# GpSimd's product of a unit's query features with the reciprocals in two halves, all low halves on VectorE, the sums of keys masked, and a new table of order corrections

## The chip, the cores and the metric

The kernel runs on one core of a Trainium2 chip. The metric is the device time of one execution in microseconds (us), the median of several runs: 1688.12 us over three runs of the kernel before (1687.51 to 1689.02). Five engines work side by side, each through its own queue in a fixed order: PE (TensorE, matrix products), DVE (VectorE), ACT (ScalarE), POOL (GpSimd) and SP (SyncE, which here issues all transfers). An instruction that has to wait holds up everything behind it on its engine.

## The reference

Two attention layers over 2048 tokens, 1024 wide, 32 heads of 32, whose outputs are laid side by side. Layer A works in four segments of 512 tokens: causal softmax attention inside a segment, plus a memory that is carried from segment to segment. Layer B is linear attention with learned features:

```python
pq = einsum("bhsd,hdf->bhsf", q, w_phi)            # the same for k
phi_q = concat([softmax(pq), softmax(-pq)], -1)    # 64 features a head
phi_k = concat([softmax(pk), softmax(-pk)], -1)
kv = einsum("bhsf,bhsd->bhfd", phi_k, v);  z = einsum("bhsf->bhf", phi_k)
o = einsum("bhqf,bhfd->bhqd", phi_q, kv) / (phi_q . z + 1e-6)
```

Then `o @ wo`. The change touches layer B's `kv` and its queries.

## The kernel before

Every large product is done with operands split into a high and a low half of 16 bits (high times high, high times low, low times high), so nearly every tile that PE reads has been written twice: ACT writes the high half, then DVE or POOL writes the low half as the difference of the value and its high half. Products of 1024 by 1024 by a pair of token tiles are done with seven block products (`strassen`, line 618 for the matmuls, 624 and 628 for the sums between them).

Four stages follow one another on PE. **Units** (to about 900 us): 32 units of layer A (four heads of a segment each), with the projections of the next unit (line 404), the scores twice (lines 882 and 983, once for the maxima, which DVE reduces at line 888, and once for the exponentials, lines 987 to 990) and the product with the values (line 1019). Between them lies work in advance for layer B: folded weights, and the prepared forms of pairs of token tiles (`prepare`, whose maxima DVE takes at line 1174). **Keys** (to about 1205 us): for each of eight pairs of token tiles the key features and values of layer B, summed into `kva` and `ez` (line 1444) and `za`. **Queries** (to about 1540 us): 16 token tiles c, each in two half-units hb of 16 heads. **Output** of layer A (line 1681) to the end.

A half-unit of the queries is a chain. PE's `strassen` gives the scores; DVE takes maxima and minima (1274), subtracts them (1276, 1278), ACT takes exponentials (1281), DVE sums them and takes reciprocals (1284, 1287). POOL multiplies with the sums of keys `zb` (1587, two instructions), DVE reduces (1590), three small steps of POOL and DVE give the reciprocal of the denominator (1593 to 1598), POOL multiplies the features `e` with these reciprocals (1600, one instruction over 1024 columns), ACT writes the high half into `S` (1607, two instructions of 512), and the low half is written by line 1610, two instructions of 512: by DVE, but for the first two token tiles the second of the two by POOL. SP then issues a transposing transfer into `pt` (1613), and PE multiplies with `kls` (1622, 48 small matmuls). After both half-units ACT and DVE bring the result out of PSUM into `ot` (1631, 1633) and PE projects it (line 404, 48 matmuls a token tile).

`kls` is `kva` and `ez`, each multiplied with reciprocals of the sums of keys (`zr`, lines 1471 to 1476), in two halves of 16 bits (1478, 1480). Its blocks hold two heads by two heads; line 1622 reads only the two blocks on the diagonal.

The order of every queue is worked out in Python when the program is built. Each `op(...)` names its engine, an assumed duration, what it reads and writes, and a due number `prio`. `Graph.run` then goes through the engines, and of the instructions that could start earliest on one it takes that of the lowest due number. Instructions with the same due number that follow each other in the text are a job; a table `MOVES` adds a correction to the due numbers of single jobs on single engines:

```python
        if prio != self.job[0]:
            self.job = prio, self.job[1] + 1
        prio += MOVES.get(eng, {}).get(self.job[1], 0.0)
```

Of the kernel before, what the change touches and what calls it, by code (L numbers as in the profile page):

```python
# [8 lines left out]
F32 = mybir.dt.float32  # L9
# [67 lines left out]
    "ACT": {  # L77
# [6 lines left out]
    "POOL": {  # L84
        42: 1, 95: -4, 100: -5, 147: 2, 148: -1.5, 150: -5, 161: 0.5, 173: 12, 188: 7, 222: -21.5, 240: 2.6, 245: 0.5,
        250: -1.5, 255: -2.5, 257: -2.5, 264: -5.5, 270: -5, 282: -22.5, 326: -8, 328: 2, 341: -2.5, 376: 10.5, 389: -36.5},
# [205 lines left out]
def tile_kernel(ctx: ExitStack, tc: tile.TileContext, ax, aw, awv, awo, beta, bx, bwqk, bwv, bphi, bwo, out):  # L292
# [37 lines left out]
    nc.vector.memset(one, 1.0)  # L330
    pst = const.tile([128, NT // 2, 5], F32, name="pst")
# [958 lines left out]
    def bc32(r):  # L1290
        return r()[:, :, :, None].to_broadcast([128, 16, 2, 32])
# [177 lines left out]
    for hb in range(2):  # L1469
        zr, v = G.buf("b", [128, 8], F32, "zr", 2), slice(8 * hb, 8 * hb + 8)  # L1470
# [5 lines left out]
        op(DVE, 0.62, lambda zr=zr, hb=hb: nc.vector.tensor_tensor(  # L1476
            kva[hb](), kva[hb](), zr()[:, :, None].to_broadcast([128, 8, 64]), op=OP.mult), r=[zr], w=[kva[hb]], prio=P, port=True)
# [75 lines left out]
    for c in range(NT):  # L1553
# [28 lines left out]
        for hb in range(2):  # L1582
            e, r = er[c % 2, hb]
            dn = G.buf("b", [128, 16, 2], F32, "dn", 2)
            for a in range(2):
# [14 lines left out]
            op(POOL, 1.95, lambda e=e, r=r: nc.gpsimd.tensor_tensor(e(), e(), bc32(r), op=OP.mult),  # L1600
               r=[e, r], w=[e], prio=P)
# [4 lines left out]
            for q in range(2):  # L1606
                op(ACT, 0.53, lambda q=q, e=e, hv=hv: nc.scalar.activation(
                    hv()[:, 0, 512 * q:512 * q + 512], ev(e)[:, 512 * q:512 * q + 512], AF.Copy), r=[e], w=[(eh, (hb, 0, q))], prio=P)
                sub, ns, d = (POOL, nc.gpsimd, 1.28) if q and c < 2 else (DVE, nc.vector, 0.7)
                op(sub, d, lambda q=q, e=e, hv=hv, ns=ns: ns.tensor_tensor(  # L1610
                    hv()[:, 1, 512 * q:512 * q + 512], ev(e)[:, 512 * q:512 * q + 512], hv()[:, 0, 512 * q:512 * q + 512], op=OP.subtract),
                   r=[e, (eh, (hb, 0, q))], w=[(eh, (hb, 1, q))], prio=P, port=True)
# [140 lines left out]
```

## Time and profile before

| | us |
|---|---|
| median of 3 runs | 1688.12 |
| the profiled execution, whole | 1690.85 |
| its span, from first to last instruction | 1689.1 |
| PE busy in it | 1658.1 |
| DVE busy | 1344.2 |
| ACT busy | 1157.4 |
| POOL busy | 966.5 |

The profiled execution is 2.7 us longer than the median; sums below are made against it and then carried to the median as differences. Busy time of PE counts a matmul to its modelled end, so a PE that is busy is not always one at full pace. The second part of the page shows the busy share of each engine in 40 slices and the clock that PE was granted; a table by stretches of time, asked of the trace, shows what each engine did in each stage.

### The profile page before, as it was taken

To read this page: it belongs to the slowest core of one execution; us is meant where nothing else is said; L and a number is where in the kernel's file an instruction comes from. 1 tells how busy PE (TensorE), PEld (TensorE's weight loads), DVE (VectorE), ACT (ScalarE), POOL (GpSimd) and SP (SyncE) were. 2 spreads that over 40 slices of the span, in tenths; PEclk is the share of its full clock that TensorE was granted. 3 is DMA by queue.
4 is the path that set the end of the run, shared out by engine and by line. 5 is a ranking of instruction groups with operands and counts; after the bars stand their busy time and mean duration, and the time that the engine had idled before them with its cause. 6 is when DMAs were issued, how large, how long until landed. Compare 5 with 4: busy or idle time off the path is not lost. (4 is left out here: it accounts for less than half of the span.)

```text
span 1689.1 us, 40231 instructions
## 1 busy us (share of the span) xinstructions
PE 1658.1 (98%) x15176; PEld 995.5 (59%) x15176; DVE 1344.2 (80%) x3198; ACT 1157.4 (69%) x2128; POOL 966.5 (57%) x1285
## 2 busy tenths in 40 slices
PE   8999999999999999999999999999979999999999
PEld 6767667666767767767764454454534444444444
DVE  6889898888998878878974787877978896976441
ACT  7898989878878988777873486765545564454331
POOL 4346578546468885756661576754588888450000
PEclk9999999999999999999999999999989999999999
DMA  7556646655766484864367465467546775865311
GB/s 224 170 170 165 211 141 195 210 174 160 243 195 191 140 223 126 224 188 127 93 179 265 150 219 168 139 205 282 207 97 166 173 202 136 220 140 169 124 57 62
DMA packets 261970, 292.64 MB, mean 173 GB/s; under 512 B 138880, under 2 KB 192896, under 8 KB 255120
## 3 DMA queue, kind: packets, MB, share of 16 engines
q1 hardware_dynamic: 261776, 290.07, 57.5%
q8 instruction: 119, 1.95, 0.5%
q14 instruction: 75, 0.61, 0.1%
HBM read 161.17 MB, written 86.05 MB: 146 GB/s over the span
## 5 line engine op out<-in xcount | busy, mean ns | idle before, releaser
L404 PE MATMUL proj<-S,S 128*128 128x512 f16 (+1 forms) x3072 | 504.3, 300 | 2.8 <-ACT S L437 1.1
L404 PEld LDWEIGHTS <-S 128*128 128x128 f16 x4608 | 333.8, 98 | 154.0 <-issue 7.4
L618 PE MATMUL proj<-S,S 128*128 128x512 f16 x1584 | 362.7, 379 | 0.6 <-ACT cs L624 0.6
L618 PEld LDWEIGHTS <-S 128*128 128x128 f16 x2016 | 192.8, 98 | 220.4 <-issue 1.8
L996 POOL TENSOR_SCALAR_AFFINE_SELECT ph<-ph 128x256 f16<-128x256 f16 (+1 forms) x448 | 192.1, 451 | 139.1 <-DVE ph L990 113.4
L888 DVE CUSTOM_DVE_ANT_0 s<-s,causal 128x256 f32<-128x256 f32 (+3 forms) x512 | 242.7, 509 | 16.7 <-PE s L882 13.3
L990 DVE SCALAR_TENSOR_TENSOR ph<-s,ph 128x512 f16<-128x512 f32 x320 | 209.7, 682 | 40.5 <-ACT ph L989 38.7
L989 ACT ACTIVATE ph<-s 128x512 f16<-128x512 f32 x320 | 189.1, 649 | 0.7
L404 PE MATMUL misc<-S,ot 128*128 128x512 f16 x768 | 175.2, 385 | 0.7 <-ACT ot L1631 0.7
L1281 ACT ACTIVATE e<-e,sk 128x256 f32<-128x256 f32 x256 | 112.3, 496 | 61.5 <-DVE e L1278 59.7
L404 PEld LDWEIGHTS <-ot 128*128 128x128 f16 x768 | 74.4, 99 | 90.7 <-issue 3.4
L983 PE MATMUL s<-S 104*128 104x512 f16 (+3 forms) x512 | 115.7, 299 | 1.9 <-ACT S L910 1.2
L882 PE MATMUL s<-S 96*128 96x512 f16 (+3 forms) x512 | 112.9, 299 | 2.3 <-DVE mt L888 1.4
L987 ACT ACTIVATE s<-s,os 128x512 f32<-128x512 f32 x160 | 105.5, 700 | 13.7 <-PE s L983 13.6
L987 ACT ACTIVATE s<-s,bd 128x512 f32<-128x512 f32 x160 | 106.2, 705 | 7.9 <-PE s L983 6.5
L404 PE MATMUL proj<-wv,S 128*128 128x128 f16 x1536 | 108.4, 219 | 0.0
L1019 PEld LDWEIGHTS <-ph 128*128 128x128 f16 x2560 | 87.1, 96 | 18.0 <-issue 1.9
L1587 POOL TENSOR_TENSOR e<-e,zb 128x512 f32<-128x512 f32 x64 | 84.7, 1341 | 21.8 <-DVE r L1284 18.2
L1019 PE MATMUL pv<-vl,ph 128*128 128x66 f16 (+1 forms) x2560 | 91.9, 184 | 1.0 <-DVE mt L888 0.6
L1284 DVE TENSOR_REDUCE r<-e 128x32 f32<-128x1024 f32 x64 | 76.7, 1205 | 16.3 <-ACT e L1281 16.3
L888 DVE DVE_READ_ACCUMULATOR2_ANT mt<- 128x1 f32 x512 | 72.0, 141 | 0.0
L1393 POOL TENSOR_TENSOR e<-e,r 128x1024 f32<-128x1024 f32 x32 | 61.3, 1920 | 15.4 <-DVE r L1287 11.9
(336 smaller groups left out, 3257.1 us busy)
## 6 DMA issues: line engine op xcount, KB each, us to landing
S<-xf_d SPq DMA_DIRECT2D x126, 256.0 KB
S<-h SPq DMA_DIRECT2D x192, 128.0 KB
S<-wf_d SPq DMA_DIRECT2D x21, 1024.0 KB
st<-bwqk SPq DMA_DIRECT2D x64, 256.0 KB
out<-os SPq DMA_DIRECT2D x40, 256.0 KB
S<-aw SPq DMA_DIRECT2D x16, 512.0 KB
wa_d<-S SPq DMA_DIRECT2D x16, 512.0 KB
wf_d<-fo SPq DMA_DIRECT2D x32, 256.0 KB
```

Source lines behind the costliest of these rows:

```text
L404: op(PE, dur, lambda c=c, a=a, b=b, lv=lv, rv=rv: nc.tensor.matmul(pv(), lv(), rv(), start=(c == 0 and a + b == 0), stop=(c == n - 1 and a ...
L618: op(PE, 0.215, lambda n=n, a=a, b=b, lv=lv, rv=rv: nc.tensor.matmul(ps(), lv(), rv(), start=(start and n == 0 and a + b == 0), stop=(n == ...
L882: nc.tensor.matmul(ps()[:, o:o + 128 * i + 128], st()[0:96, 0, h, 128 * i:128 * i + 128], st()[0:96, 1, h, 0:128 * i + 128], start=True, s ...
L888: dve(0.12 + 0.00113 * n, lambda h=h, i=i, o=o, n=n: nc.vector.tensor_tensor_reduce(ps()[:, o:o + n], ps()[:, o:o + n], causal[:, 512 - n: ...
L983: nc.tensor.matmul(ps()[:, o:o + n], st()[0:104, 1, h, 128 * j:128 * j + 128], st()[0:104, 0, h, 128 * j:512], start=True, stop=True)
L987: act(0.59, lambda: nc.scalar.activation(ps(), ps(), AF.Exp, bias=0.0, scale=bdv()[:, 3, i2, 0:1]), r=[(bd, i2)], w=[ps])
L989: act(0.5, lambda: nc.scalar.activation(ph()[:, 0], ps(), AF.Copy, scale=2.0 ** 14), r=[ps], w=[(ph, 0)])
L990: dve(0.6, lambda: nc.vector.scalar_tensor_tensor(ph()[:, 1], ps(), 2.0 ** 14, ph()[:, 0], op0=OP.mult, op1=OP.subtract), r=[ps, (ph, 0)], ...
L996: nc.gpsimd.affine_select(pd, pd, pattern=[[0, n], [1, 128]], compare_op=OP.is_ge, fill=0.0, base=0, channel_multiplier=-1)
L1019: nc.tensor.matmul(ps()[:, i, n0:n1], ph()[:, a, o:o + 128], vl()[:, j, h, n0:n1], start=(i == 0 and a == 0), stop=(j == min(i, 2)), skip_ ...
L1281: op(ACT, 0.41, lambda i=i: nc.scalar.activation(e()[:, 4 * i:4 * i + 4], e()[:, 4 * i:4 * i + 4], AF.Exp, bias=0.0, scale=sk()[:, i:i + 1 ...
L1587: op(POOL, 1.35, lambda a=a, h0=h0, e=e: nc.gpsimd.tensor_tensor(e()[:, 8 * a:8 * a + 8], e()[:, 8 * a:8 * a + 8], zv()[:, h0:h0 + 8], op= ...
```

## The change

Four edits. First, the product of line 1600 becomes two instructions of 512 columns, and each half of ACT's and DVE's work waits for its own half alone. Second, all low halves of the queries are DVE's. Third, `zr` is multiplied with a mask `bm2` (1 on the two diagonal blocks, 0 elsewhere) into `zs`, a small tile of 8 by 2, and `kva` and `ez` are multiplied with that; the blocks that become zero are those that line 1622 doesn't read. `bm2` itself is one small reduction of DVE at the start. Fourth, the whole table `MOVES` is another one, with 167 entries in place of 234, and so the order of all five queues is worked out anew, from the first units to the end of the queries.

```diff
 MOVES = {
     "DVE": {
-        4: -4.5, 10: -1.5, 15: -4, 27: 0.5, 37: -2, 39: -45.5, 43: -22, 56: 4, 73: 0.6, 81: 7, 88: -43.5, 91: -10, 93: -48.5,
+        4: -3.5, 10: -0.5, 16: 3, 24: -0.7, 27: -0.1, 89: -0.5, 100: -2, 105: -7, 109: 1.5, 121: 0.5, 128: -2, 139: 1.1,
...
+    bm2 = const.tile([128, 2], F32, name="bm2")
+    nc.vector.tensor_reduce(bm2, bm.rearrange("p (two h) -> p two h", two=2), axis=AX.X, op=OP.add)
...
-        op(DVE, 0.62, lambda zr=zr, hb=hb: nc.vector.tensor_tensor(
-            kva[hb](), kva[hb](), zr()[:, :, None].to_broadcast([128, 8, 64]), op=OP.mult), r=[zr], w=[kva[hb]], prio=P, port=True)
+        op(DVE, 0.1, lambda zr=zr, zs=zs: nc.vector.tensor_tensor(
+            zs(), zr()[:, :, None].to_broadcast([128, 8, 2]), bm2[:, None, :].to_broadcast([128, 8, 2]), op=OP.mult),
+           r=[zr], w=[zs], prio=P)
+        op(DVE, 0.62, lambda zs=zs, hb=hb: nc.vector.tensor_tensor(
+            kva[hb]().rearrange("p g (b d) -> p g b d", d=32), kva[hb]().rearrange("p g (b d) -> p g b d", d=32),
+            zs()[:, :, :, None].to_broadcast([128, 8, 2, 32]), op=OP.mult), r=[zs], w=[kva[hb]], prio=P, port=True)
...
-            op(POOL, 1.95, lambda e=e, r=r: nc.gpsimd.tensor_tensor(e(), e(), bc32(r), op=OP.mult),
-               r=[e, r], w=[e], prio=P)
+            for q in range(2):
+                op(POOL, 1.05, lambda q=q, e=e, r=r: nc.gpsimd.tensor_tensor(
+                    e()[:, 8 * q:8 * q + 8], e()[:, 8 * q:8 * q + 8], bc32(r)[:, 8 * q:8 * q + 8], op=OP.mult),
+                   r=[e, r], w=[(e, ("y", q))], prio=P)
...
-                    hv()[:, 0, 512 * q:512 * q + 512], ev(e)[:, 512 * q:512 * q + 512], AF.Copy), r=[e], w=[(eh, (hb, 0, q))], prio=P)
-                sub, ns, d = (POOL, nc.gpsimd, 1.28) if q and c < 2 else (DVE, nc.vector, 0.7)
-                op(sub, d, lambda q=q, e=e, hv=hv, ns=ns: ns.tensor_tensor(
+                    hv()[:, 0, 512 * q:512 * q + 512], ev(e)[:, 512 * q:512 * q + 512], AF.Copy), r=[(e, ("y", q))], w=[(eh, (hb, 0, q))], prio=P)
+                op(DVE, 0.7, lambda q=q, e=e, hv=hv: nc.vector.tensor_tensor(
                     hv()[:, 1, 512 * q:512 * q + 512], ev(e)[:, 512 * q:512 * q + 512], hv()[:, 0, 512 * q:512 * q + 512], op=OP.subtract),
-                   r=[e, (eh, (hb, 0, q))], w=[(eh, (hb, 1, q))], prio=P, port=True)
+                   r=[(e, ("y", q)), (eh, (hb, 0, q))], w=[(eh, (hb, 1, q))], prio=P, port=True)
```

Three places of the new order are shown here, since the prediction rests on them. Line numbers in the rows of the change are its own: 1614 is the transposing transfer (1613 before), 1611 DVE's low half (1610), 1609 ACT's high half (1607), 1170 the maxima of a prepared pair (1174), 986 the low half of the exponentials (990).

**DVE, at the start of the queries.** Before, the rows down to the low halves of the first token tile's second half-unit (its first half-unit's stands 22 rows higher); `mx`, `r`, `d` and `dn` are the small tiles of the chain above, `S` the tile that the transfer reads:

```order
L1595 TENSOR_REDUCE d_19811<-dn 128x16
L1274 TENSOR_REDUCE mx<-proj 128x16 x2
L1284 TENSOR_REDUCE r<-e 128x32
L1274 TENSOR_REDUCE mx<-proj 128x16
L1597 RECIPROCAL d_19811<-d_19811 128x16
L1287 RECIPROCAL r<-r 128x32
L1274 TENSOR_REDUCE mx<-proj 128x16
L1610 TENSOR_TENSOR S_19649<-e,S_19649 128x512
L1480 TENSOR_TENSOR kls<-ez,kls 128x512
L1610 TENSOR_TENSOR S_19649<-e,S_19649 128x512
```

And in the change:

```order
L1283 RECIPROCAL r<-r 128x32
L415 RECIPROCAL wsc<-wsc 128x1
L1270 TENSOR_REDUCE mx<-proj 128x16
L1529 TENSOR_TENSOR wsc<-wsc,osc_109 128x1
L1270 TENSOR_REDUCE mx<-proj 128x16
L1590 TENSOR_REDUCE dn<-e 128x16
L1611 TENSOR_TENSOR S_19616<-e,S_19616 128x512 x4
L1272 TENSOR_TENSOR e<-s,mx 128x16x32
```

All four low halves of the first token tile now stand in one row, and none stands ahead of them.

**SP, at the same place**: the transfers into `pt` among the loads of token forms. Before:

```order
L606 DMA S_13808<-xf_d 128x1024
L1613 DMA_TRANSPOSE pt<-S_19649 128x16x128
L606 DMA S_13808<-xf_d 128x1024
L606 DMA S_15069<-xf_d 128x1024
L1613 DMA_TRANSPOSE pt<-S_19649 128x16x128 x3
L606 DMA S_13808<-xf_d 128x1024 x2
```

And in the change:

```order
L602 DMA S_13941<-xf_d 128x1024 x2
L1614 DMA_TRANSPOSE pt<-S_19616 128x16x128 x2
L602 DMA S_15202<-xf_d 128x1024
L1614 DMA_TRANSPOSE pt<-S_19616 128x16x128 x2
L1500 DMA out<-os 128x512 x2
```

The first token tile's two transfers are now issued one right after the other. On PE 1548 matmuls of line 618 stand ahead of the first 48 of line 1622 where there were 1540; then come 96 of line 1622 and 48 of line 404, where there were 48, 8 more of line 618, 96 and 10.

**DVE, in the units**: the first prepared pair's maxima (`xt`). Before, they stand between the `mh` (line 903) of the fourth unit and that of the fifth:

```order
L902 TENSOR_SCALAR mh<-mt 128x4x4
L1174 TENSOR_REDUCE xt<-S_2044 128x1
L1127 TENSOR_SCALAR quad<-misc,sif 128x512
L990 SCALAR_TENSOR_TENSOR ph<-s,ph 128x512 x2
L1174 TENSOR_REDUCE xt<-S_2044 128x1
L990 SCALAR_TENSOR_TENSOR ph<-s,ph 128x512
```

And in the change, between that of the third and that of the fourth:

```order
L832 SCALAR_TENSOR_TENSOR h_1865<-proj,bd,h_1865 128x512
L1170 TENSOR_REDUCE xt<-S_1925 128x1
L986 SCALAR_TENSOR_TENSOR ph<-s,ph 128x512 x3
L435 SCALAR_TENSOR_TENSOR S_1805<-S_1541,wgs,S_1805 128x512 x2
L1019 TENSOR_REDUCE oall<-pv 128x132
L986 SCALAR_TENSOR_TENSOR ph<-s,ph 128x512 x3
L1170 TENSOR_REDUCE xt<-S_1925 128x1
```

The two instructions have moved one unit ahead, to where unit work and weight halves (line 435, 439 before) already stand. The table moves such work for later stages in most units, on all engines.

More of the change, by code (lines that the diff above doesn't have):

```diff
@@ L58 @@
     "DVE": {
[18 rows of a table removed]
-    "ACT": {
[6 rows of a table removed]
[14 rows of a table added]
+    "ACT": {
[4 rows of a table added]
     "POOL": {
-        42: 1, 95: -4, 100: -5, 147: 2, 148: -1.5, 150: -5, 161: 0.5, 173: 12, 188: 7, 222: -21.5, 240: 2.6, 245: 0.5,
-        250: -1.5, 255: -2.5, 257: -2.5, 264: -5.5, 270: -5, 282: -22.5, 326: -8, 328: 2, 341: -2.5, 376: 10.5, 389: -36.5},
+        73: 0.5, 86: -0.5, 102: -3, 128: -3, 131: 1, 147: 0.1, 201: 0.1, 225: -3, 254: -2, 276: -4, 298: -27, 362: -9.5,
+        365: 1.5, 374: 1, 387: -55.5},
 }
@@ L1469, in tile_kernel @@
     for hb in range(2):
-        zr, v = G.buf("b", [128, 8], F32, "zr", 2), slice(8 * hb, 8 * hb + 8)
+        zr, zs, v = G.buf("b", [128, 8], F32, "zr", 2), G.buf("b", [128, 8, 2], F32, "zs", 2), slice(8 * hb, 8 * hb + 8)
         op(DVE, 0.1, lambda zr=zr, v=v: nc.vector.tensor_scalar(zr(), za()[:, v], 1e-12, None, op0=OP.max),
```

38 rows, old and new, of the table MOVES are left out of this document.

## The prediction

> **What bounds the kernel now.** I read the page's first two parts, then the table by stretches of time, PE's waits, and the timeline where the waits lie.
>
> ```profile
> span 1689.1 us, 40231 instructions
> PE 1658.1 (98%) x15176; PEld 995.5 (59%) x15176; DVE 1344.2 (80%) x3198; ACT 1157.4 (69%) x2128; POOL 966.5 (57%) x1285
> PEclk9999999999999999999999999999989999999999
> ```
>
> PE is busy for 98% of the span, at full clock but for one slice. Only its 31 us of idle time, and what follows from them, can be won; and as PE's work stays the same, whatever a new order adds as idle time is lost. Where the idle time lies is told by the stretches (start:end, length, then busy time of PE, PE's weight loads, DVE, ACT, POOL, granted clock, DMA share, GB/s):
>
> ```profile
> 50.00:200.00 150.00, 149.59 (x1635) 108.82 (x1633) 134.22 (x406) 133.38 (x243) 77.03 (x140) 1.00 0.57 161
> 200.00:300.00 100.00, 95.95 (x1077) 69.04 (x1075) 93.17 (x258) 90.14 (x164) 77.37 (x111) 1.00 0.59 187
> 300.00:900.00 600.00, 595.66 (x6472) 417.92 (x6473) 513.79 (x1470) 491.19 (x877) 389.58 (x592) 1.00 0.59 176
> 900.00:1205.00 305.00, 304.18 (x2078) 153.03 (x2077) 229.74 (x408) 190.66 (x391) 168.76 (x163) 1.00 0.60 205
> 1205.00:1260.00 55.00, 44.41 (x390) 21.36 (x390) 45.77 (x86) 24.31 (x50) 41.65 (x44) 0.88 0.55 150
> 1260.00:1500.00 240.00, 240.00 (x2195) 111.23 (x2194) 202.34 (x335) 125.37 (x242) 182.18 (x190) 1.00 0.69 174
> 1500.00:1550.00 50.00, 47.62 (x394) 21.65 (x393) 35.88 (x56) 22.74 (x37) 9.50 (x12) 0.97 0.61 177
> ```
>
> In the units (50 to 900 us) PE is idle for 0.4 + 4.0 + 4.3 = 8.8 us, nearly half of it between 200 and 300. Keys: 0.8 us. The start of the queries: 10.6 us, the one large hole; their middle: none; their end: 2.4 us. The hole is a wait for transposing transfers:
>
> ```profile
> PE pv L1622 <- DMA pt<-S: 11.3, 3, 7.4
> 1227.00 1.91 SPq L1613 DMA_TRANSPOSE pt<-S  x1
> 1235.69 1.15 POOL L1610 TENSOR_TENSOR S<-e,S 128x512 f16<-128x512 f32 x1
> 1238.70 1.18 DVE L1610 TENSOR_TENSOR S<-e,S 128x512 f16<-128x512 f32 x1
> 1239.94 10.83 SPq L1613 DMA_TRANSPOSE pt<-S  x3
> 1244.54 0.63 PEld L1622 LDWEIGHTS <-kls 64*32 64x32 f16 x48 [7.39 <-issue]
> 1247.61 0.57 PEld L1622 LDWEIGHTS <-kls 64*32 64x32 f16 x47 [2.43 <-issue]
> 1248.38 4.45 PE L404 MATMUL misc<-S,ot 128*128 128x512 f16 x10
> 1502.82 10.53 PE L404 MATMUL misc<-S,ot 128*128 128x512 f16 x48
> ```
>
> The second half-unit's low half by POOL is done at 1236.84; DVE's comes at 1238.70, as DVE's queue has it behind other work. The transfer is issued at 1239.94 and used at 1244.54, 4.6 us later. After the hole ten matmuls take 4.45 us, where 48 take 10.53 (0.22 each): another 2.3 us, by a lower clock. So hole and slow restart cost 7.4 + 2.4 + 2.3 = 12.1 us.
>
> **The change, part by part.**
>
> *The start of the queries.* Up to the row of four low halves DVE has, counted over its order, two L1274 and one each of L1276, L1278, L1284, L1287, L1595, L1597 fewer than up to the late low half now, and no low half ahead of them where there was one; it has one L1480 and the two masks' products more.
>
> ```profile
> L1274 DVE TENSOR_REDUCE mx<-proj 128x16 f32<-128x512 f32 x10 | 6.5, 668 | 0.1
> L1284 DVE TENSOR_REDUCE r<-e 128x32 f32<-128x1024 f32 x5 | 6.0, 1196 | 0.0
> L1278 DVE TENSOR_TENSOR e<-mx,proj 128x512 f32<-128x512 f32 x4 | 2.7, 674 | 0.0
> L1287 DVE RECIPROCAL r<-r 128x32 f32<-128x32 f32 x6 | 1.8, 318 | 0.0
> L1597 DVE RECIPROCAL d<-d 128x16 f32<-128x16 f32 x4 | 0.9, 226 | 0.0
> L1480 DVE TENSOR_TENSOR kls<-ez,kls 128x512 f16<-128x512 f32 x1 | 0.7, 678 | 0.0
> L1476 DVE TENSOR_TENSOR kva<-kva,zr 128x512 f32<-128x512 f32 x1 | 0.9, 903 | 0.0
> L1610 DVE TENSOR_TENSOR S<-e,S x60: 628/710/2396, 1225.3 to 1519.4; 128x512 f16<-128x512 f32 x60
> ```
>
> Less: 2 x 0.67 + 2 x 0.67 + 1.20 + 0.32 + 0.23 + 0.71, and for L1595 no more than the 0.23 of L1597: 5.4 us. More: 0.68, and two products of 16 columns, which the trace doesn't have; between nothing and an L1287 (0.32), I take 0.2 each: 1.1 us. The product of kva itself keeps its 512 columns and so its 0.7 to 0.9. DVE is busy for 45.8 of these 55 us, so the row begins about 4.3 us sooner, at 1234.4, and its four parts, 0.7 each, end at 1235.8 for the first half-unit and 1237.2 for the second. SP issues the first transfer at about 1236 and, 1.9 us later, the second at 1238; 4.6 us on, PE has them at 1240.7 and 1242.8. By now the second is used at 1244.54: 1.7 us won. The wait of 2.43 us for the next tile goes, since 48 matmuls of the projection (10.5 us) now stand ahead of it; but these wait for `ot`, four evictions after the last small matmul, and that wait is open where now 48 small matmuls stand (0.6 us). From 1244.54 to 1248.38 pass 3.8 us now; from 1242.8 the projection begins at 1246.6 at the latest: 1.8 us won, 0.6 of it owed for the 48 that come later. Term: -1.2 us. Bounds: -12.1 if the hole goes altogether, +2.8 if DVE's row is not sooner and its four parts come on top.
>
> A rule of the Trainium skill (page "SBUF — State Buffer", section "SBUF: two separate sides") speaks against this part: a VectorE instruction with two inputs in SBUF and a GpSimd instruction that reads SBUF share one pair of ports, as a lock held for a whole instruction, and the loser stands still. The trace agrees, with 2396 ns at most beside the median 710 in the last row above; had each of the four parts the 0.5 us more of the row at 1238.70, the term would be +0.8.
>
> *The halves on POOL.*
>
> ```profile
> L1600 POOL TENSOR_TENSOR e<-e,r x32: 1903/1912/2363, 1222.3 to 1513.6; 128x1024 f32<-128x1024 f32 x32
> L1587 POOL TENSOR_TENSOR e<-e,zb x64: 1255/1270/1804, 1204.8 to 1498.5; 128x512 f32<-128x512 f32 x64
> L1610 POOL TENSOR_TENSOR S<-e,S x4: 1154/1270/1450, 1225.7 to 1247.7; 128x512 f16<-128x512 f32 x4
> ```
>
> A half of 512 columns costs between 0.96 (half of 1.91) and 1.27 (L1587, as many columns). It is the same operation as L1600, so I take 1.0: 64 x 1.0 - 32 x 1.91 = +3 us on POOL, up to +20 by the other bound, less 4 x 1.27 = 5 for the low halves that leave. Between 1260 and 1500 POOL has 58 of 240 us free and PE waits for nothing: no cost there. What a half-unit wins is that ACT begins one half, 0.9 us, sooner; it counts only where PE waits.
>
> *The end of the queries.*
>
> ```profile
> 1516.33 4.51 PE L404 MATMUL misc<-S,ot 128*128 128x512 f16 x13 [0.70 <-ACT ot L1631]
> ```
>
> The idle 2.4 us and 4.51 - 13 x 0.22 = 1.7 us of slow restart are 4.1 us. In the order of the change POOL's last four halves stand in a row, behind the small steps of both half-units, and 15 matmuls (3.3 us) stand on PE between the last two products where there were 24 (5.3 us). Two half-units that end together, with shorter cover: I take -1.0, bounds -4.1 and +4.
>
> *The new order elsewhere.* PE's idle time in the units is not where ACT or DVE has most to do alone, but where the order leaves no spare:
>
> ```profile
> 100.00:150.00 50.00, 49.69 (x526) 34.23 (x524) 46.10 (x152) 43.22 (x78) 27.38 (x44) 1.00 0.71 183
> 150.00:200.00 50.00, 49.90 (x580) 37.75 (x578) 46.16 (x130) 45.43 (x83) 28.74 (x52) 1.00 0.58 166
> 400.00:450.00 50.00, 49.65 (x514) 35.52 (x513) 48.76 (x151) 40.86 (x76) 26.19 (x48) 1.00 0.73 231
> 450.00:500.00 50.00, 50.00 (x565) 35.68 (x563) 47.29 (x129) 40.17 (x72) 30.20 (x49) 1.00 0.64 183
> L1174 DVE TENSOR_REDUCE xt<-S x10: 1192/1205/1215, 151.2 to 746.5; 128x1 f32<-128x1024 f32 x10
> ```
>
> Three stretches of 100 us have DVE at 92 of 100 or more: 100 to 200 (92.3), 200 to 300 (93.2), 400 to 500 (96.1). The first and the last lose 0.4 and 0.35 us, the middle one 4.0. Only the sequence keeps the two tight ones quiet, and the change draws it anew: the first pair's two maxima (2 x 1.2 us) now at 151 move a unit ahead, into the stretch 100 to 150, onto a DVE with 3.9 of 50 us free. I take it that these two come to lose what 200 to 300 loses: 2 x 4.05 - 0.76 = +7.3 us. Bounds: -8.8 if the new order has no idle time in the units, +25.6 if all 850 us lose 4.05 in 100 (34.4 - 8.8). In keys, middle and output, idle for 0.8 us now, an order can only lose; I take once more the 0.8 of the keys.
>
> Sum: -1.2 - 1.0 + 7.3 + 0.8 = +5.9 us. On the profiled execution (span 1689.1, 1690.85 with what lies around it) that is 1696.8; it stood 2.7 above the median, so on the median 1688.1 it is **1694**.
>
> **The rivals.**
>
> *The order is better, not worse* (faster). The units' chain would lose nothing in the tight stretches and 4 us less between 200 and 300, and the start of the queries half of its 12.1: 1688.1 - 4 - 6 = 1678; with the tail's 1.0, 1677. For it: 31 us of idle time are there, and low halves that no longer wait for both POOL and DVE. Against: POOL's low half was done 1.9 us ahead of DVE's, so it was never POOL that held the transfer. It decides where the first four low halves end before 1232.5, 4.6 us ahead of the time at which PE runs dry now (1244.54 - 7.39 = 1237.1).
>
> *Nothing moves.* The masked blocks have no reader, and the halves serve a chain that PE doesn't wait for in 240 of 300 us; start -1.2, tail -1.0 and a units' loss of 2 cancel: 1688. That the edits don't do what they say is in this case.
>
> *DVE and POOL block one another* (slower still). Low halves between 1260 and 1500 are covered by PE's full queue, but at both ends each of eight loses 0.5 us and POOL's last four halves cost 1.27: 4 + 1.2, on top of the forecast 1694 + 5 = 1699; decided by whether low halves in the row of four exceed 1.1 us.
>
> **How the numbers follow.** Forecast 0.50, faster rival 0.25, nothing 0.17, blocked ports 0.08. A measurement of this kernel tells about 0.2%, 3.4 us, from no change. Forecast and blocked ports lie beyond it: slower 0.58; same 0.17; faster 0.25. The likeliest case's own range is 1691 to 1706. The range has to reach into the faster rival, half of which lies above 1677, and up to half of the units' upper bound (1688 + 20): 1677 to 1708.
>
> **What would show it.** The table by stretches: PE idle above 10 us in 50 to 900, most of it in 100 to 200 and 400 to 500; 8 to 10 us idle around the first transfers, without the second wait; no idle between 1260 and 1500. Low halves in a row near 0.7 us, POOL's halves near 1.0. Wrong it would be if the units' idle time fell below 8.8 us, or if PE's wait for the first transfers were under 4 us or over 11.

## The result and the profile after

| | before | after |
|---|---|---|
| median of 12 runs, us | 1688.87 (1685.5 to 1691.3) | 1692.48 (1690.3 to 1696.6) |
| profiled span, us | 1689.1 | 1691.9 |
| ratio after to before | | 1.0023, 95% interval 1.0014 to 1.0032 |

The changed kernel is slower by 0.23%, 3.6 us; the forecast was 5.9 us. The first lines of its page:

```profile
span 1691.9 us, 40286 instructions
PE 1658.1 (98%) x15176; PEld 994.2 (59%) x15176; DVE 1353.6 (80%) x3205; ACT 1154.9 (68%) x2128; POOL 980.3 (58%) x1313
```

PE is busy for the same 1658.1 us, so the 2.8 us that the span has grown by are idle time. Where it lies is told by the table by stretches (start:end, length, then busy time of PE, weight loads, DVE, ACT, POOL, granted clock, DMA share, GB/s) of the changed kernel:

```profile
50.00:200.00 150.00, 148.79 (x1626) 107.67 (x1624) 129.17 (x391) 126.32 (x231) 74.42 (x135) 1.00 0.51 154
200.00:300.00 100.00, 95.33 (x1002) 68.57 (x1000) 92.21 (x250) 93.67 (x170) 75.59 (x105) 0.98 0.58 180
300.00:500.00 200.00, 193.26 (x2167) 136.37 (x2165) 184.13 (x510) 161.42 (x289) 111.74 (x186) 1.00 0.64 197
500.00:900.00 400.00, 398.09 (x4331) 278.84 (x4330) 332.55 (x969) 324.75 (x584) 274.39 (x405) 1.00 0.56 164
900.00:1205.00 305.00, 304.96 (x2048) 151.77 (x2045) 226.53 (x406) 187.97 (x388) 177.85 (x172) 1.00 0.61 207
1205.00:1260.00 55.00, 45.78 (x380) 24.04 (x379) 53.76 (x102) 28.17 (x57) 35.50 (x41) 0.94 0.57 167
1260.00:1500.00 240.00, 239.52 (x2284) 111.15 (x2283) 206.80 (x334) 127.18 (x247) 194.68 (x218) 1.00 0.69 173
1500.00:1550.00 50.00, 49.18 (x409) 22.46 (x407) 38.73 (x62) 24.50 (x40) 15.68 (x19) 1.00 0.62 173
```

In the units (50 to 900 us) PE is now idle for 1.2 + 4.7 + 6.7 + 1.9 = 14.5 us, 5.7 more than before. At the start of the queries it is 9.2 us (10.6 before), at their end 0.8 (2.4 before), and at both ends the clock stays higher: 0.94 for 0.88 and 1.00 for 0.97. What the queries won is less than what the units lost.

The units also lost some clock, which they had not before: between 200 and 300 us it is 0.98 for 1.00, and all of that lies in the last ten of these (0.83 between 290 and 300), right behind PE's longest wait in the stretch, which ends with ACT:

```profile
PE misc L931 <- ACT oT L670: 1.9, 1, 1.9
```

A clock that is 0.17 short for 10 us is, as an estimate, another 1.7 us lost beside the idle time.

The three places that the forecast spoke of read as follows in the changed kernel. First its timeline at the start of the queries (start, length, instruction): DVE's row of four low halves, POOL's halves beside it, the transfers, and PE's weight loads that wait for them:

```profile
1242.03 4.37 DVE L1611 TENSOR_TENSOR S<-e,S 128x512 f16<-128x512 f32 x4
1242.24 1.50 POOL L1601 TENSOR_TENSOR e<-e,r 128x512 f32<-128x512 f32 x1
1244.36 1.49 POOL L1601 TENSOR_TENSOR e<-e,r 128x512 f32<-128x512 f32 x1
1244.35 4.61 SPq L1614 DMA_TRANSPOSE pt<-S  x2
1248.97 0.47 PEld L1623 LDWEIGHTS <-kls 64*32 64x32 f16 x48 [2.25 <-issue]
1251.77 0.57 PEld L1623 LDWEIGHTS <-kls 64*32 64x32 f16 x47 [2.33 <-issue]
1253.46 1.03 PE L400 MATMUL misc<-S,ot 128*128 128x512 f16 x2 [0.85 <-ACT ot L1632]
1254.91 7.32 PE L400 MATMUL misc<-S,ot 128*128 128x512 f16 x29 [0.42 <-DVE ot L1634]
```

The two waits for transfers are 2.25 and 2.33 us where they were 7.39 and 2.43. They are not the same two: before, the second was for the next token tile, and now it stands between the two half-units of the first. The first two matmuls of the projection take 1.03 us and the 29 behind them 7.32, together 1.5 more than 31 x 0.22; before, ten lost 2.3. But the low halves take 1.09 us each, not 0.7, and each half on POOL beside them 1.5.

Second, the same stretch for PE by what it waited for (total, times, longest):

```profile
PE pv L1623 <- DMA pt<-S: 4.5, 2, 2.3
PE misc L1454 <- DVE za L1440: 1.8, 1, 1.8
PE proj L614 <- ACT cs L620: 1.4, 2, 0.8
PE misc L400 <- ACT ot L1632: 0.9, 1, 0.9
```

So 5.2 us of the old hole's 9.8 are gone, but of the 9.2 us that PE is idle in this stretch 4.6 are now waits for other things, where there were 0.8: for the sums of keys `za`, for the sums `cs` inside `strassen`, and for `ot`.

Third, the units, in the stretches where the forecast expected the loss and those where it was:

```profile
100.00:150.00 50.00, 50.00 (x565) 35.03 (x563) 47.24 (x148) 43.55 (x79) 28.38 (x47) 1.00 0.50 147
150.00:200.00 50.00, 49.51 (x569) 36.84 (x568) 40.26 (x115) 40.42 (x74) 22.85 (x47) 1.00 0.49 147
350.00:400.00 50.00, 47.59 (x492) 31.99 (x490) 44.79 (x119) 45.20 (x83) 26.69 (x44) 1.00 0.65 201
400.00:450.00 50.00, 46.57 (x533) 34.65 (x529) 48.42 (x139) 36.57 (x67) 21.36 (x41) 1.00 0.58 172
```

DVE is busier between 100 and 150 than before (47.2 of 50) and PE loses nothing there; between 150 and 200 DVE has 5.9 us less to do than before (40.3 for 46.2). Most of the loss stands between 350 and 450: 2.4 + 3.4 us, where it was 1.1 + 0.35.

### The profile page after: what moved, and what is told of

Its sections match the earlier page's. It is cut to its first block, busy times and chain, and to the rows that moved or that the text cites. A ratio compares the mean times of both kernels' runs of the same rounds, so it can differ in the third digit from the quotient of the medians.

```text
span 1691.9 us, 40286 instructions
## 1 busy us (share of the span) xinstructions
PE 1658.1 (98%) x15176; PEld 994.2 (59%) x15176; DVE 1353.6 (80%) x3205; ACT 1154.9 (68%) x2128; POOL 980.3 (58%) x1313
## 4 chain that ended last, share of the span: by engine, by line
PE 61%; DVE 11%; ACT 2%; issue 1%; POOL 1%; DMA 1%; DVEq 0%; ACTq 0%; POOLq 0%
PE proj L614 16%; PE proj L400 12%; PE misc L400 9%; PE proj L1682 5%; PE s L614 3%; PE s L1682 2%; PE pv L1015 2%; PE s L979 2%; PE misc L614 2%; PE s L878 2%; DVE s L884 2%; DVE ph L986 1%; DVE S L1611 1%; PE misc L1682 1%; PE kv L1431 1%; DVE mx L1270 1%
## 5 line engine op out<-in xcount | busy, mean ns | idle before, releaser
L400 PE MATMUL proj<-S,S 128*128 128x128 f16 (+1 forms) x3072 | 497.7, 300 | 2.4 <-ACT S L433 1.1
L884 DVE CUSTOM_DVE_ANT_0 s<-s,causal 128x512 f32<-128x512 f32 (+3 forms) x512 | 241.8, 509 | 11.4 <-PE s L878 8.3
L983 ACT ACTIVATE s<-s,os 128x512 f32<-128x512 f32 x160 | 106.7, 715 | 10.7 <-PE s L979 10.4
L983 ACT ACTIVATE s<-s,bd 128x512 f32<-128x512 f32 x160 | 106.8, 709 | 10.2 <-PE s L979 10.1
L1587 POOL TENSOR_TENSOR e<-e,zb 128x512 f32<-128x512 f32 x64 | 85.0, 1343 | 10.6 <-DVE r L1280 9.7
L1611 DVE TENSOR_TENSOR S<-e,S 128x512 f16<-128x512 f32 x64 | 66.4, 1069 | 9.2 <-ACT S L1609 8.8
L1601 POOL TENSOR_TENSOR e<-e,r 128x512 f32<-128x512 f32 x64 | 72.7, 1145 | 1.5
```

The lines of the kernel that those rows point to most:

```text
L400: op(PE, dur, lambda c=c, a=a, b=b, lv=lv, rv=rv: nc.tensor.matmul(pv(), lv(), rv(), start=(c == 0 and a + b == 0), stop=(c == n - 1 and a ...
L884: dve(0.12 + 0.00113 * n, lambda h=h, i=i, o=o, n=n: nc.vector.tensor_tensor_reduce(ps()[:, o:o + n], ps()[:, o:o + n], causal[:, 512 - n: ...
L983: act(0.59, lambda: nc.scalar.activation(ps(), ps(), AF.Exp, bias=0.0, scale=bdv()[:, 3, i2, 0:1]), r=[(bd, i2)], w=[ps])
```

## The experiments

Twelve kernels, each beside runs of the kernel before. "The old table" is the `MOVES` of before, "the new" that of the change (counted in the two kernels they have 260 and 171 entries, not 234 and 167); jobs 0 to 236 belong to the units and their work in advance, jobs 237 to 398 to what follows.

| kernel | median, us | ratio to before, 95% interval |
|---|---|---|
| after | 1692.5 | 1.0023 (1.0014 to 1.0032) |
| units_old | 1685.4 | 0.9985 (0.9976 to 0.9994) |
| units_new | 1721.1 | 1.0192 (1.0178 to 1.0205) |
| edits_only | 1698.4 | 1.0057 (1.0045 to 1.0069) |
| table_only | 1697.1 | 1.0052 (1.0040 to 1.0064) |
| halves_only | 1706.6 | 1.0104 (1.0090 to 1.0118) |
| low_only | 1700.2 | 1.0068 (1.0055 to 1.0080) |
| units_old_one | 1704.9 | 1.0100 (1.0085 to 1.0116) |
| units_mid | 1707.0 | 1.0109 (1.0090 to 1.0129) |
| edits_old_order | 1691.8 | 1.0016 (1.0007 to 1.0025) |
| halves_old_order | 1688.7 | 0.9997 (0.9987 to 1.0007) |
| one_new_order | 1686.7 | 0.9985 (0.9976 to 0.9994) |
| short_maxima | 1691.5 | 1.0014 (1.0004 to 1.0023) |

### Which half of the new table costs

**units_old**: the changed kernel with the old corrections of jobs 0 to 236, on all engines.

```diff
 MOVES = {
     "DVE": {
-        4: -3.5, 10: -0.5, 16: 3, 24: -0.7, 27: -0.1, 89: -0.5, 100: -2, 105: -7, 109: 1.5, 121: 0.5, 128: -2, 139: 1.1,
+        4: -4.5, 10: -1.5, 15: -4, 27: 0.5, 37: -2, 39: -45.5, 43: -22, 56: 4, 73: 0.6, 81: 7, 88: -43.5, 91: -10, 93: -48.5,
...
-        160: -2, 161: 4.5, 172: -7.5, 196: 0.5, 203: -2, 219: -2, 222: 6.5, 225: -20, 240: -9.5, 254: -3, 257: -0.5, 261: -6.5,
+        214: 1.5, 219: 6, 220: 2.5, 225: 2.5, 240: -9.5, 254: -3, 257: -0.5, 261: -6.5, 268: -3.5, 284: -8.5, 287: -4, 292: -4, 294: -1,
...
```

> All edits of the change, but the corrections of the jobs that belong to the units and the work in advance (jobs 0 to 236) are those of before; so the order up to the keys is the old one and the order behind it the new one. Theory (the new order of the units loses, the new start and end of the queries win): PE's idle time between 50 and 900 us falls back from 14.5 to about 8.8 us, the queries keep their 9.2 + 1.3 us, and the time is 4 to 6 us below before: 1683 to 1685 where before is 1688.9. Rival (the loss comes from the edits in the queries: halves on POOL, low halves on DVE): the time stays at that of the change, 1692 or above.

**units_new**: the other way round, old corrections from job 237 on.

```diff
-        160: -2, 161: 4.5, 172: -7.5, 196: 0.5, 203: -2, 219: -2, 222: 6.5, 225: -20, 240: -9.5, 254: -3, 257: -0.5, 261: -6.5,
+        161: 4.5, 172: -7.5, 196: 0.5, 203: -2, 219: -2, 222: 6.5, 225: -20, 240: 2, 245: 1, 247: 2, 250: -14, 270: -6.5, 272: -13,
...
```

> All edits of the change, the new corrections for the units (jobs 0 to 236), the old ones from the keys on (jobs 237 to 398). Theory: the units lose as in the change (idle 14 to 15 us between 50 and 900), and the queries have no order drawn for the edits: 6 to 9 us above before, 1695 to 1698. Rival (the units' order is worth nothing, the queries decide): within 2 us of before.

units_old came to 1685.4 us, 0.4 above the theory's range and far from the rival's 1692: 3.3 us below before and 7.1 below the change. Its profiled execution took 1682.0 us, 3.4 less than its median, so the idle times in its table by stretches are those of a good execution:

```profile
200.00:300.00 100.00, 97.40 (x1116) 70.82 (x1116) 93.22 (x263) 91.20 (x167) 76.73 (x112) 1.00 0.58 183
300.00:500.00 200.00, 198.50 (x2135) 139.58 (x2133) 181.04 (x492) 166.10 (x295) 110.34 (x179) 1.00 0.65 199
1205.00:1260.00 55.00, 47.77 (x397) 22.17 (x396) 51.28 (x92) 29.48 (x59) 39.61 (x45) 0.94 0.54 150
1500.00:1550.00 50.00, 49.14 (x409) 22.38 (x407) 34.64 (x52) 24.84 (x41) 5.82 (x6) 1.00 0.58 169
```

Between 300 and 500 PE is idle for 1.5 us instead of 6.7, and the queries keep their gain. The two orders of the units show the same in other kernels: with the old one PE is idle for 6.8 to 9.0 us between 50 and 900 (nine profiles, that of before among them; DVE, ACT and POOL have one and the same sequence there up to 939 us), with the new one for 14.5 to 15.6 (after, units_new, table_only).

units_new missed its 1695 to 1698 by far. The units lose what was expected (15.3 us idle), but the old corrections of the queries do not fit work that arrives at other times. PE's waits:

```profile
PE pv L1626 <- DMA pt<-S: 17.9, 5, 12.1
PE pv L1626 <- ACT kls L1481: 10.2, 1, 10.2
```

`kls` itself comes late by 10.2 us, a wait that neither kernel has. A table's two halves are no independent terms.

### Edits against table

**edits_only** is the changed kernel with the whole old table, **table_only** the kernel before with the whole new one. The diff is that of edits_only; for table_only its signs are turned.

```diff
 MOVES = {
     "DVE": {
-        4: -3.5, 10: -0.5, 16: 3, 24: -0.7, 27: -0.1, 89: -0.5, 100: -2, 105: -7, 109: 1.5, 121: 0.5, 128: -2, 139: 1.1,
+        4: -4.5, 10: -1.5, 15: -4, 27: 0.5, 37: -2, 39: -45.5, 43: -22, 56: 4, 73: 0.6, 81: 7, 88: -43.5, 91: -10, 93: -48.5,
...
```

> The three edits with the whole old table. Theory: units as before (idle 8.8 us between 50 and 900); the edits alone are worth -3 to +3 us, as the low half that POOL had for the second half-unit was not the late one: 1686 to 1692. Rival (the edits cost): above 1692, with the wait for the first transfers longer than 7.4 us.

> None of the three edits, only the new table. Theory: units lose as in the change (idle 14 to 15 us), and the start of the queries is no better than before since the product of 1024 columns on POOL and POOL's low halves are back: 1692 to 1698. Rival (the edits cost): below the change, 1688 to 1690.

edits_only was 9.7 us slower than before, so the rival's number, but not in the rival's place: the start of the queries has 10.1 us idle, as before, and the whole loss stands in the last stretch:

```profile
1205.00:1260.00 55.00, 44.87 (x386) 0.88 0.53 148
1500.00:1550.00 50.00, 38.75 (x397) 0.86 0.61 168
```

(The columns are PE's busy time, clock, DMA share and GB/s.) At the end of its queries ACT's timeline shows

```profile
1523.70 1.15 ACT L1618 ACTIVATE S<-e 128x512 f16<-128x512 f32 x2 [6.69 <-DMA pt<-S]
```

The high halves of the last half-unit wait for a transfer that still reads from `S`. That transfer had been issued late: the work on two half-units stands mixed on POOL, ACT and DVE, four low halves come between 1512.2 and 1519.0, and the two transfers go out one right behind the other, at 1519.1 and 1521.0. table_only came out in the theory's range and lost the units' 15.6 us idle too, and 5.1 us at the end of the queries; but its start of the queries has 7.7 us idle, less than the change, where the theory saw no gain. So the gain at the start is the new order's, not the edits'.

### One edit at a time, order drawn anew

**halves_only** and **low_only**: the kernel before, the old table, one edit each.

```diff
-            op(POOL, 1.95, lambda e=e, r=r: nc.gpsimd.tensor_tensor(e(), e(), bc32(r), op=OP.mult),
-               r=[e, r], w=[e], prio=P)
+            for q in range(2):
+                op(POOL, 1.05, lambda q=q, e=e, r=r: nc.gpsimd.tensor_tensor(
+                    e()[:, 8 * q:8 * q + 8], e()[:, 8 * q:8 * q + 8], bc32(r)[:, 8 * q:8 * q + 8], op=OP.mult),
+                   r=[e, r], w=[(e, ("y", q))], prio=P)
```

> The kernel before with the old table and one edit alone: POOL's product in two halves of 512, ACT's and DVE's halves each waiting for its own. Theory (the halves break the old order at the end of the queries, where the two last half-units' instructions come to stand between one another): the wait for one of the last two transfers is 8 to 10 us as with all three edits and the old table, start of the queries as before: 1697 to 1699. Rival (the end is lost by the low halves or the mask): 1688 to 1690, last waits together under 3 us.

```diff
-                sub, ns, d = (POOL, nc.gpsimd, 1.28) if q and c < 2 else (DVE, nc.vector, 0.7)
+                sub, ns, d = DVE, nc.vector, 0.7
```

> The kernel before with the old table and one edit alone: the low halves of the first two token tiles all on DVE. Theory: they are not what the first transfer waits for, four more low halves of DVE cost at most 4 x 0.7 us: 1688 to 1692, end of the queries as before. Rival (DVE's row is what breaks): above 1695.

**units_old_one**: units_old with the product in one piece (the first diff reversed). **units_mid**: units_old with the new corrections from job 122 on.

> As units_old (all edits, old corrections to job 236, new ones behind), but POOL's product again one instruction of 1024 columns. Theory (edit and new table fit one another; without the halves the chain of the last half-units is later by about 0.9 us each and the new order has it otherwise): the end of the queries loses 2 to 8 us: 1688 to 1693. Rival (the new order alone makes the gain, the halves nothing): 1685, within 1.5 us of units_old.

```diff
 MOVES = {
     "DVE": {
-        4: -3.5, 10: -0.5, 16: 3, 24: -0.7, 27: -0.1, 89: -0.5, 100: -2, 105: -7, 109: 1.5, 121: 0.5, 128: -2, 139: 1.1,
+        4: -4.5, 10: -1.5, 15: -4, 27: 0.5, 37: -2, 39: -45.5, 43: -22, 56: 4, 73: 0.6, 81: 7, 88: -43.5, 91: -10, 93: -48.5,
...
-        160: -2, 161: 4.5, 172: -7.5, 196: 0.5, 203: -2, 219: -2, 222: 6.5, 225: -20, 240: -9.5, 254: -3, 257: -0.5, 261: -6.5,
+        96: -9, 98: -35, 100: -8.5, 104: -43.5, 106: -12.5, 112: -9.5, 114: -23.5, 118: 4.5, 121: -13, 128: -2, 139: 1.1, 160: -2, 161: 4.5,
...
```

> As units_old, but the new corrections already from job 122 on, which is about the middle of the units. Theory (what the new order of the units loses lies between 200 and 500 us, and behind 500 it is some 2 us better): idle time of PE up to 500 us as before, 500 to 900 us at 2.0 us or less in place of 2.4 to 2.7, 1683 to 1685. Rival (the new corrections of the second half rest on the new order of the first): idle time of 4 us or more behind 500 us, 1687 or above.

All four lost 12 to 22 us against the kernel that they start from; all four theories missed in the time, and the rivals' bounds were met in low_only and units_mid. halves_only has the expected wait of 9 us at the end, but also 6.8 us idle between 1260 and 1500 where before has none, and at the start of the queries PE waits 8.1 us for `kls` and only 1.3 for the transfers. halves_only and low_only each cost more than the three edits together (18.0 and 11.6 against 9.7 us), so these are not prices of edits. In low_only most of the loss stands at the start of the queries (18.1 us idle for 10.6), as two timelines of DVE and POOL show:

```profile
1238.17 3.78 POOL L1603 TENSOR_TENSOR e<-e,r 128x1024 f32<-128x1024 f32 x2
1240.78 5.66 DVE L1613 TENSOR_TENSOR S<-e,S 128x512 f16<-128x512 f32 x4 [0.15 <-ACT S L1610]
1241.91 3.38 POOL L1590 TENSOR_TENSOR e<-e,zb 128x512 f32<-128x512 f32 x2
```

The planner put four low halves in one row, and POOL's products stand beside them without a pause: 5.66 us for four, 1.42 each. The transfer of the second half-unit is issued at 1246.6 (1239.94 before), and PE's longest wait is 14.8 us. units_mid has 6.0 us idle between 500 and 900 us, where the orders that it was joined from have 1.9 and 2.4.

In three of the four the planner's input changed and the corrections did not; in units_mid it is the corrections alone that changed. That suggests the order, not the instruction, as the price; the next three test it.

### The edits with an order that stays

The planner is given the instructions of one kernel while the instructions of another are emitted at their places. So all queues keep their order but for the instruction that is split or replaced.

**edits_old_order**: all three edits in the order of before.

```diff
-            op(POOL, 1.95, lambda e=e, r=r: nc.gpsimd.tensor_tensor(e(), e(), bc32(r), op=OP.mult),
+            op(POOL, 1.95, lambda e=e, r=r: [nc.gpsimd.tensor_tensor(
+                e()[:, 8 * q:8 * q + 8], e()[:, 8 * q:8 * q + 8], bc32(r)[:, 8 * q:8 * q + 8], op=OP.mult) for q in range(2)],
                r=[e, r], w=[e], prio=P)
...
-                op(sub, d, lambda q=q, e=e, hv=hv, ns=ns: ns.tensor_tensor(
+                op(sub, d, lambda q=q, e=e, hv=hv: nc.vector.tensor_tensor(
```

> All three edits, but the planner sees the instructions of before, so that every queue keeps the order of before: the two halves on POOL stand where the one product stood, the four low halves stand in DVE's queue at the time at which POOL had them, the small product with the mask stands ahead of that of kva. Theory (the edits themselves are worth little; what cost 10 to 18 us in the kernels with the old table was that the planner draws a new order for every change of its input): within 3.5 us of before, 1685 to 1692. Rival (the edits as such cost): 1697 or above, as with the order that the planner draws for them.

**halves_old_order** has the first of these two pieces alone.

> As edits_old_order, with the halves on POOL alone. Theory: 0 to 3 us below before (ACT can begin 0.9 us sooner in the few places where PE waits): 1685 to 1689, against 1706.6 for the same edit with the order that the planner draws. Rival (the second instruction on POOL costs): above 1692.

**one_new_order**: the order of units_old, the product whole.

```diff
-                op(POOL, 1.05, lambda q=q, e=e, r=r: nc.gpsimd.tensor_tensor(
-                    e()[:, 8 * q:8 * q + 8], e()[:, 8 * q:8 * q + 8], bc32(r)[:, 8 * q:8 * q + 8], op=OP.mult),
+                op(POOL, 1.05, lambda q=q, e=e, r=r: None if q else nc.gpsimd.tensor_tensor(
+                    e(), e(), bc32(r), op=OP.mult),
```

> The order of units_old in every queue, but POOL's product again in one instruction of 1024 columns, at the place of the first half. Theory: the halves are worth at most the 0.9 us that ACT begins sooner at each place where PE waits, 0 to 3 us: 1685 to 1689. Rival (the halves are what the new order gains by): 1695 or above, as when the planner draws the order for the whole product (1704.9).

All three came out where the theory had them. The halves alone, in an order that stays, are worth nothing that can be measured: 1688.7 us (ratio 0.9997) where the drawn order gave 1706.6; and undone in the new order they leave 1686.7, the same ratio 0.9985 as units_old. Low halves and mask together cost 1691.8 - 1688.7 = 3.1 us in the old order. Their place, in the timeline of DVE in edits_old_order:

```profile
1237.41 1.60 DVE L1619 TENSOR_TENSOR S<-e,S 128x512 f16<-128x512 f32 x1
1238.93 1.53 DVE L1488 TENSOR_TENSOR kls<-ez,kls 128x512 f16<-128x512 f32 x1
1240.39 1.53 DVE L1619 TENSOR_TENSOR S<-e,S 128x512 f16<-128x512 f32 x1
```

and the row of the same kernel in the table by stretches:

```profile
1205.00:1260.00 55.00, 41.57 (x364) 19.37 (x364) 47.83 (x86) 23.10 (x48) 36.29 (x44) 0.84 0.47 134
```

PE is idle for 13.4 us at the start of the queries, 2.8 more than before: two low halves and the low half of `kls` between them take 1.5 to 1.6 us each beside a busy POOL, where such a low half takes 0.68 us beside an idle one and the one at this place took 1.18 before. The mask alone was not tried.

### What PE waits for between 300 and 500 us

**short_maxima**: the changed kernel in its own order, twelve of DVE's maxima shortened.

```diff
-                    tw()[:, 2 * j + k:2 * j + k + 1], t()[:, k], axis=AX.XY, op=OP.max, apply_absolute_value=True),
+                    tw()[:, 2 * j + k:2 * j + k + 1], t()[:, k, :, :64], axis=AX.XY, op=OP.max, apply_absolute_value=True),
...
-                        tw()[:, k:k + m], v(), axis=AX.X, op=OP.max, apply_absolute_value=True), r=rs, w=[(tw, k)], prio=prio)
+                        tw()[:, k:k + m], v()[:, :, :64] if m > 1 else v(), axis=AX.X, op=OP.max, apply_absolute_value=True), r=rs, w=[(tw, k)], prio=prio)
```

> The changed kernel in its own order, but twelve maxima of DVE between 300 and 500 us (eight of 1024 columns, 1.2 us each, and four of 2048 columns, 2.3 us each) taken over an eighth of their columns, some 16 us of DVE's 184 less; the scales come from these columns alone. Theory (between 300 and 500 us PE waits because DVE, with work in advance, has no spare time): PE's idle time there falls from 6.7 us to 3 us or less, the time to 1687 to 1690. Rival (PE waits there for chains whose length DVE's load does not set): idle 5.5 us or more, time within 1.5 us of the change.

PE's idle time there fell from 6.7 to 4.5 us, between the two theories, and the time by 1.0 us, which is within the rival's bound and, as the intervals overlap, not clear of noise. PE's waits in that stretch say why. In the changed kernel all the long ones end with DVE:

```profile
PE misc L1120 <- DVE amem L938: 1.6, 1, 1.6
PE s L979 <- DVE ph L986: 1.5, 2, 1.2
PE pv L1015 <- DVE oall L1019: 0.9, 1, 0.9
PE misc L904 <- DVE mh L899: 0.9, 2, 0.7
```

and in short_maxima the second is one that did not exist:

```profile
PE misc L1122 <- DVE amem L940: 1.2, 1, 1.2
PE s L880 <- ACT vf L814: 0.9, 1, 0.9
PE s L981 <- DVE ph L988: 0.8, 1, 0.8
```

With 10.7 us less of DVE's work (173.5 for 184.1), what ends with DVE is about halved, and 1.2 us now end with ACT. So DVE's work in advance is part of the cause; the rest lies in the sequence, and which instructions it lies in stays open.

## Why the prediction was right

The direction was right, and so was the balance behind it: a new order of the units loses more than the queries win. The terms came out as follows.

**Order elsewhere (+7.3 in the units): size right, place wrong.** The two orders of the units differ by 1692.5 - 1685.4 = 7.1 us on the chip, where each of the two times is uncertain by some 1.5 us; in the profiles of before and after it is 5.7 us of idle time and an estimated 1.7 us of slower clock, a term that the working did not have. But the loss did not come as the working had it: that made 100 to 200 and 400 to 500 lose what 200 to 300 loses. The two maxima that moved into 100 to 150 cost nothing (PE busy for 50.0 of 50), and most of the loss lay between 300 and 500, 3.1 us of it in the stretch 400 to 500 that was named. That the sum agrees to 0.2 us owes something to chance. The price of 4.05 us in 100 was itself no constant: in nine profiles with the same order of the units, 200 to 300 lost 2.6 to 4.1 us.

**Start of the queries (-1.2): the way right, the gain too small.** The row of low halves did begin sooner. Counted from the end of the last matmul of the keys (line 1435, 1431 in the change; at 1207.2 before and 1215.9 after), it begins after 26.1 us and the first transfer is issued after 28.4; the working had 27.2 and 28.8, and the late low half and its transfer stood at 31.5 and 32.8 before. Idle time fell by 1.4 us. The four low halves cost 1.09 us each, not the 0.7 taken; 0.5 more was named as what the rule of the Trainium skill (page "SBUF — State Buffer", section "SBUF: two separate sides") would make of them. The traces agree that both engines lose: beside the row POOL's halves take 1.5 us for 1.05. Whether a whole instruction is the span of the lock no run here shows. The price did not decide: the wait for the next token tile went as forecast, though another of 2.33 us came in between the two half-units, and the working left out that less would be lost to the slow clock behind the hole, 1.5 us where 2.3 were.

**End of the queries (-1.0): right in sign, too small.** The idle time fell by 1.6 us, and the slow restart of 1.7 us is gone. The keys lost nothing (305.0 of 305 us busy), so their +0.8 fell away as well. From units_old, where the units are as before, both ends and the keys together are worth -3.3 us by the medians, -1.0 to -4.1 by its interval; the working had -1.2 - 1.0 + 0.8 = -1.4. In the profiles of before and after, idle time behind the units (900 to 1550 us) fell by 3.2 us. So this is the mis-sized part of the sum, though the interval of units_old alone would still admit -1.4. That 7.1 and -3.3 together give about the measured 3.6 is no check, since they come from the same medians.

**Halves on POOL at no cost: right.** The row of the changed kernel for that line (shortest, median, longest in ns, first and last start):

```profile
L1601 POOL TENSOR_TENSOR e<-e,r x64: 1044/1049/1522, 1227.9 to 1516.5; 128x512 f32<-128x512 f32 x64
L1611 DVE TENSOR_TENSOR S<-e,S x64: 625/850/1825, 1242.0 to 1522.4; 128x512 f16<-128x512 f32 x64
```

A half takes 1.05 us at the median against 1.0 taken, and halves_old_order moves by 0.15 us. All 64 took 73.3 us of POOL where the 32 whole products took 62.8: 10.5 more, not the 3 of the working, but within its bound of 20. The low halves' median went from 710 to 850 ns, hidden behind PE's full queue in the middle, which lost 0.5 us.

**The rivals.** The faster one was half right: a better order was there for the queries, but its price of 10 us was too high and the units spoiled it; the first four low halves, which it needed done before 1232.5, ended at 1246.4. It looked for the gain in low halves that no longer wait for both engines; edits_old_order shows the three edits to be a loss of 3.0 us without a new order. *Nothing moves* fell, by little more than the 0.2% that it allowed. *DVE and POOL block one another* set 1.1 us a low half as its point, and they reached 1.09; but of the 5 us that it put at the two ends nothing is seen in the total, since both ends won.

**The signs.** Above 10 us idle in the units held (14.5), and so did 8 to 10 us around the first transfers (9.2); the stretches named for the units' loss were wrong in part, the middle lost 0.5 us where no loss was expected, and low halves took 1.09 us for 0.7. PE's wait for the first transfers, 4.6 us in all, came close to the 4 below which the forecast called itself wrong.

**A bound that does not follow.** The upper end of the range, 1688 + 20, was to be half of the units' upper bound; half of 25.6 is 12.8, which gives 1701 and not 1708. The measured time lies within both.

## A version that beats both

units_old keeps the old order up to the keys and the new one behind: 1685.4 us, 0.15% (0.06 to 0.24%) below before and 7.1 us below the change. one_new_order, with the product whole, can't be told from it.

## What to carry to other kernels

Where a planner draws the order, an edit has two prices: that of its instructions in an order that stays, and that of the order that is drawn for it; here they were 0 and 18 us for the same edit, so measure them apart, by letting the planner see the old instructions. A table of corrections belongs to the input that it was made for and is not to be cut or joined unmeasured, though one joint, at the boundary of two stages, held (units_old); the same joint the other way round cost 32 us (units_new). And when a hole in PE's work opens or closes, count the slow restart behind it too: in this case it was 1.5 to 2.3 us behind the holes at the start of the queries.

## What the runs showed of the hardware

A DVE low half (two inputs of 512 columns) takes 0.68 us beside an idle POOL (before), 1.09 us beside POOL's products in the row of the changed kernel, 1.42 in low_only, where POOL has no pause, and POOL's product of 512 columns takes 1.5 for 1.05. Splitting POOL's product did not shorten this: beside one product of 1024 columns the row of four took 4.25 us (one_new_order), beside two halves 4.37 (the change), in one profile each. The granted clock fell behind waits of PE in the units and in the queries alike: 0.83 over 10 us behind a wait of 1.9 us, 0.88 over the 55 us with the hole of 7.4 and 2.4 us. Profiles of one and the same order in the units differ by up to 2.2 us of idle time (6.8 to 9.0), so a difference of a microsecond in one stretch of one profile is no evidence.
